# Two fp32 buffers for x and another way to place the first state, in an attention and feed-forward kernel

## The chip, the core and the metric

The kernel runs on one core of one Trainium2 chip. The metric is the device time of one execution, in microseconds. Each run has a state: it counts as slow when it is more than 1.5% above the fastest run of the same kernel, or ran at a clock lowered throughout; ratios use fast runs only. For before, whose fastest run took 218.28 us, runs up to 221.5 us still count as fast. Engines: PE multiplies matrices, PEld is its weight load, DVE the vector engine, ACT the scalar engine, POOL the general engine that also issues software DMAs, SP the engine that issues nearly all the other DMAs (its queue is shown as SPq).

## The reference, cut to what matters

```python
B, H, S, Ns, D = 8, 8, 512, 32, 64          # x: (B,H,S,D), state: (B,H,Ns,D)
scores = x @ state.T / sqrt(D);  a = softmax(scores);   xread = a @ state
scores2 = state @ x.T / sqrt(D); a2 = softmax(scores2); sread = a2 @ x
h_in = concat([xread, sread], axis=2)       # 544 rows per batch, 512 wide
g = silu(h_in @ w_in)                       # 512 -> 2048
out = g @ w_out                             # 2048 -> 512, 4352 rows
```

The kernel works batch by batch. For the 512 x rows of a batch it folds `state @ w_in` into one matrix W of the batch ("G1" multiplies by W, "G2" by w_out; `aT`, the transposed softmax weights, is the other operand of G1). `ft` counts the 16 tiles of the 2048-wide middle layer. So PE has some 23 us of dense matmuls for each batch.

## The kernel before: the parts that matter

Each batch's x travels a chain: load (DMA, fp32) into `x_f`, cast to bf16 into `x_nat`, transpose into `xT`, scores on PE. The kernel has one `x_f` buffer for all batches. Batches 0 and 1 are transposed on PE; from batch 2 on the DMA queues transpose.

```python
x_f = pers.tile([128, H, 4, D], FP32)                 # one buffer
def load_x(b, h0=0, nh=H):
    nc.gpsimd.dma_start(x_f[:, ds(h0, nh)], x[b, ...])
def transpose_x(b):
    nc.sync.dma_start_transpose(xT[b] ..., x_nat[b] ...)

# state of batch 0: one PE transpose, then four strided copies on ACT
ps0 = transpose_one_state(st0_n)
place_one_state(0, ps0, nc.scalar)
...
load_x(1, 0, 4); load_x(1, 4, 4); load_states()       # in the start
pe_transpose_a(0, 1, nc.vector, nc.scalar)            # aT copied in two halves
...
# batch 0, ft 13: cast x1 on DVE, then load x2 into the same x_f
for hg in range(2):
    cast_x(1, nc.vector, 0, 4, 4 * hg, 4)
load_x(2)
...
# batch 0, last quarter, ft 11
for c in range(4):
    cast_x(2, nc.gpsimd, c, 1)                        # POOL
transpose_x(2)                                        # SP queue
...
# batch 1, ft 12: scores of batch 2 on PE, then
if b == 1:
    load_x(3)                                         # POOL, once the casts of x2 freed x_f
```

Although `load_x(3)` is written in batch 1, POOL has nothing between it and the four casts of x2, so POOL issues it directly behind them (the trace below shows it there), long before PE comes to that point.

The softmax here doesn't subtract the row's maximum and nothing guards it: scores larger than these inputs give would overflow.

Of the kernel before, what the change touches and what calls it, by code (L numbers as in the profile page):

```python
# [8 lines left out]
FP32 = mybir.dt.float32  # L9
# [10 lines left out]
H = 8  # L20
S = 512
NS = 32
D = 64
# [18 lines left out]
def kernel(  # L42
# [8 lines left out]
    nc = tc.nc  # L51
    ds = bass.ds
# [3 lines left out]
    pers = ctx.enter_context(tc.tile_pool(name="pers", bufs=1))  # L56
# [15 lines left out]
    def bank(shape, dtype, name):  # L72
        tag = banks[turn[0] % len(banks)]
        turn[0] += 1
        return psA.tile(shape, dtype, tag=tag, name=name)

    ident = pers.tile([128, 128], BF16)
# [3 lines left out]
    st0_n = pers.tile([128, 2, D], BF16)  # L81
# [18 lines left out]
    xT = {}  # L100


    x_f = pers.tile([128, H, 4, D], FP32)

    def load_x(b, h0=0, nh=H):
        nc.gpsimd.dma_start(  # L106
            x_f[:, ds(h0, nh)], x[b, ds(h0, nh)].rearrange("h (p c) d -> p h c d", p=128, c=4)
        )

    def ones_beside_x(i, eng):  # L110
        eng.memset(
            x_rows[i][:, 0 : 16 * XW].rearrange("p (i w) -> p i w", w=XW)[:, :, 0:PAD], 1.0
        )
        eng.memset(x_rows[i][:, ds(16 * XW, PAD)], 1.0)

    def padded(b):
        return x_rows[b % NX][:, ds(PAD, 16 * XW)].rearrange(
            "p (c k w) -> p c k w", c=4, k=4
        )[:, :, :, 0:128]

    def cast_x(b, eng, c0=0, nc_=4, h0=0, nh=H):
        if b < 2:
            x_nat[b] = padded(b)
        elif b not in x_nat:
            x_nat[b] = xpool.tile([128, 4, 4, 128], BF16, tag="x_nat", name=f"x_nat{b}")
        copy(
            eng,
            x_nat[b][:, ds(c0, nc_), ds(h0 // 2, nh // 2), :].rearrange(
                "p c k (u d) -> p c k u d", u=2
            ),  # L130
            x_f[:, ds(h0, nh), ds(c0, nc_), :].rearrange("p (k u) c d -> p c k u d", u=2),
        )

    def transpose_x(b):
# [13 lines left out]
    def copy(eng, dst, src):  # L148
        if eng is nc.scalar:
            nc.scalar.activation(dst, src, func=COPY, bias=0.0)  # L150
        else:
            eng.tensor_copy(dst, src)  # L152


    def keep_busy(n, pool, tag):
        ps = pool.tile([128, 512], FP32, tag=tag, name="ps_busy")
        for _ in range(n):
            nc.tensor.matmul(  # L158
                ps[:], busy[:, 0:128], busy[:], start=True, stop=True, skip_group_check=True
            )  # L160
# [9 lines left out]
    nc.scalar.activation(warm[:], warm[:], func=EXP, bias=0.0)  # L170
    for hg in range(2):
        nc.sync.dma_start(
            x_f[:, ds(4 * hg, 4), :, :],
            x[0, ds(4 * hg, 4)].rearrange("h (p c) d -> p h c d", p=128, c=4),
        )
    nc.vector.memset(stT[:, 0], 0.0)
# [14 lines left out]
    def load_states():  # L191
        nc.gpsimd.dma_start(
            st_b[:], state.rearrange("b h (n2 m v) d -> (b h n2) m (v d)", n2=2, m=8)
        )

    def transpose_one_state(st):
        ps = bank([128, 2, 2, 2, 16], BF16, "ps_st1")
        nc.tensor.transpose(
            ps.rearrange("p g k u m -> p (g k u m)"), st.rearrange("p v d -> p (v d)"), ident[:]
        )  # L200
        return ps

    def place_one_state(b, ps, eng):
        flat = stT.rearrange("p b k s n -> p (b k s n)")
        to = (
            flat[0:64, ds(256 * b, 320)].rearrange("p (g w) -> p g w", g=2)[:, :, 0:128],
            flat[64:128, ds(256 * b + 32, 192)].rearrange("p (g w) -> p g w", g=2),
        )
        for u in range(2):
            by_n = to[u].rearrange("p g (k m v) -> p g k m v", m=16, v=2)  # L210
            for v in range(2):
                copy(eng, by_n[:, :, 0:3:2, :, v], ps[ds(64 * v, 64), :, :, u, :])

    keep_busy(7, psH, "h1")
    copy(nc.vector, st0_n[:], st0_f[:])
    ps0 = transpose_one_state(st0_n)
    keep_busy(2, psH, "h1")


# [14 lines left out]
                    )  # L234
            copy(engs[u], xT[b][:, ds(m * u, m), ds(2 * hg, 2), :], ps[:])

    place_one_state(0, ps0, nc.scalar)
    cast_x(0, nc.vector, 0, 2, 0, 4)
    cast_x(0, nc.scalar, 2, 2, 0, 4)
    new_o = lambda sh, dt, nm: psO.tile(sh, dt, tag="o", name=nm)  # L240
# [80 lines left out]
    def pe_transpose_a(b, hg, eng, other=None):  # L321
        ps = bank([128, 4, 128], BF16, "ps_at")
        for c in range(4):
            nc.tensor.transpose(ps[:, c, :], an[b, hg][:, c, :, :], ident[:])
        if other is None:
            copy(eng, aT[b][:, hg, :, :], ps[:])
        else:
            copy(eng, aT[b][:, hg, 0:2, :], ps[:, 0:2])
            copy(other, aT[b][:, hg, 2:4, :], ps[:, 2:4])
# [194 lines left out]
    for hg in range(2):  # L524
        load_x(1, 4 * hg, 4)
    load_states()
    for i in (1, 2):
        ones_beside_x(i, nc.gpsimd)
    keep_busy(4, psO, "o")
    pe_transpose_a(0, 0, nc.vector)  # L530
    keep_busy(1, psO, "o")
    pe_transpose_a(0, 1, nc.vector, nc.scalar)
    g1_half(0, 0)
    g1_half(1, 0)

# [7 lines left out]
    for ft in range(NFT):  # L543
        upto(min(ft + LEAD0[ft], ready))
        if ft in W0:
            w1_cols(0, [W0[ft]], both)
            ready = sum(W0[ft]) // 128
        if ft == 4:
            place_one_state(1, transpose_one_state(st1_n), nc.vector)
        if ft == 13:  # L550
            for hg in range(2):
                cast_x(1, nc.vector, 0, 4, 4 * hg, 4)
            load_x(2)
        if ft in (5, 9, 11):
            w1_chunks(1, ({5: 0, 9: 1, 11: 2}[ft],), both)
        if ft == 14:
            nc.scalar.activation(warm[:], warm[:], func=EXP, bias=0.0)
            pe_transpose_x(1, 0, 1, engs=(nc.vector,))
            pe_transpose_x(1, 1, 1, engs=(nc.vector,))
        if ft < 14:  # L560
            for tt in range(3):
                G2(0, tt, ft)
# [32 lines left out]
    for b in range(1, B):  # L595
        n = b + 1
        lead = 4 if b == 1 else 6
        for tt in range(4):
            for ft in range(NFT):
                at = (tt, ft)  # L600
                if tt == 0:
                    upto(NFT * b + min(lead + ft, NFT))
                if b == 1 and at == (0, 1):
                    transpose_state()
                    for u in range(2):
                        evict_state(u, nc.vector)
                if b == B - 1 and at in ((0, 4), (0, 8)):
                    place_xm(at[1] // 8, nc.vector)
                if n < B:
                    if at == (0, NFT - lead):  # L610
                        scores(n, 0)
                        scores(n, 1)
                        exps(n, 0)
                        exps(n, 1)
                        nc.scalar.activation(warm[:], warm[:], func=SILU, bias=0.0)  # L615
                        if b == 1:
                            load_x(3)
                    if at == (1, 0):
                        for hg in range(2):
                            norm(n, hg, (((nc.gpsimd, nc.vector)[hg], 0, 4),))  # L620
                            transpose_a(n, hg)
                        if n + 1 < B:
                            for c in range(4):
                                cast_x(n + 1, nc.gpsimd, c, 1)
                        if n + 2 < B:
                            load_x(n + 2)
                    if at == (3, 8):
                        if n + 1 < B:
                            transpose_x(n + 1)
                    if at == (0, 4):  # L630
                        copy(nc.vector, padded(n), x_nat[n][:])
                    if at == (2, 4):
                        if b == 1:
                            sread((0, 1))
                        sread((n,))
                        pss = w1_mms(n, [(0, 512), (512, 512)])
                        w1_out(n, [(0, 512)], both, pss)
                        for m in (0, 1, 2) if b == 1 else (n,):
                            sread_out(m)
                        w1_out(n, [(512, 512)], both, pss)  # L640
                    if at == (3, 4):
                        w1_chunks(n, (2, 3), both)
                    if tt == 3 and ft % 2 == 1 and ft // 2 < 6:
                        upto(NFT * n + ft // 2 + 1)
                elif tt > 0 and (ft % 3 == 2 or ft == NFT - 1):
                    upto(min(done[0] + 1, NFT * (B + 1)))
                G2(b, tt, ft)
            store(b, tt, nc.scalar if tt in (1, 2) else nc.vector)
        for ft in range(NFT):
            gt.pop(NFT * b + ft)  # L650
# [34 lines left out]
```

## Time and profile before

| | before |
|---|---|
| timed, median of the first 3 runs | 218.43 us (218.41 to 218.93) |
| the profiled run | 225.7 us, span 223.9 us, marked slow |
| PE busy in that run | 211.0 us, 94% |
| period of a later batch on PE | 22.91 us |

The page of before. The digits are tenths of busy time, or of the full TensorE clock, in 40 equal slices of the span:

```profile
span 223.9 us, 3944 instructions
...
PE   7799999983999999999999999999999999999993
...
PEclk9999999997699999999999999999999999999999
...
```

PE is full except at both ends and in slices 9 and 10; its clock is down in slices 10 and 11 (7 and 6 tenths). The waits view of PE (what waited, for what: us in total, times, longest) has one long wait:

```profile
...
PE ps_sc L279 <- DMA xT<-x_nat: 4.1, 1, 4.1
PE ps_busy L158 <- DVE warm L165: 1.2, 1, 1.2
...
```

The timeline around it (start us, length us, engine, line; in brackets the idle time before it and what ended it):

```profile
...
32.56 0.89 POOL L106 DMA_DIRECT2D x_f<-in_x_dram  x1 [16.29 <-DVE x_rows L152]
...
41.85 2.28 POOL L152 CAST x_nat<-x_f 128x512 bf16<-128x512 f32 x4 [3.79 <-DMA x_f<-in_x_dram]
...
44.16 1.79 SPq L137 DMA_TRANSPOSE xT<-x_nat  x1
...
44.43 0.93 POOL L106 DMA_DIRECT2D x_f<-in_x_dram  x1 [0.30 <-POOL x_nat L152]
...
53.91 1.04 PE L279 MATMUL ps_sc<-stT,xT 128*128 128x64 bf16 x16 [4.07 <-DMA xT<-x_nat]
...
```

This is the chain of x2: load issued at 32.56, after POOL had waited for the cast of x1; landed just before 41.85; four casts; transpose issued at 44.16; load of x3 issued 0.27 us later; scores of batch 2 at 53.91, after PE stood 4.07 us. The view of stretches (stretch and its length, busy us and count of PE, PEld, DVE, ACT, POOL, then granted clock, DMA share, GB/s) shows what followed:

```profile
...
45.00:50.00 5.00, 4.79 (x22) 1.99 (x21) 1.45 (x4) 4.60 (x9) 0.36 (x1) 1.00 1.22 154
50.00:55.00 5.00, 1.09 (x17) 0.99 (x18) 0.00 (x0) 2.21 (x3) 0.00 (x0) 0.80 0.64 215
55.00:60.00 5.00, 5.00 (x13) 1.77 (x12) 3.21 (x6) 2.12 (x4) 1.59 (x2) 0.52 0.15 56
...
```

The clock is 0.52 from 55 to 60 us. The Trainium skill, "TensorE: Matmul & The Clock Gate", Part 1, names a cause for a fall of this kind: PE's clock is halved after an idle window of about 3.4 us. Here PE stood 4.07 us.

The start, up to the first exp of batch 0:

```profile
...
4.50 0.99 ACT L150 ACTIVATE stT<-ps_st 64x64 bf16<-64x64 bf16 x4 [1.80 <-PE ps_st L198]
...
5.05 0.43 DVE L152 CAST x_rows<-x_f 128x512 bf16<-128x512 f32 x1 [1.04 <-DMA x_f<-in_x_dram]
...
5.51 0.63 ACT L150 ACTIVATE x_rows<-x_f 128x512 bf16<-128x512 f32 x1
...
7.44 0.60 ACT L293 ACTIVATE exp_nat<-ps_sc 128x512 bf16<-128x512 f32 x1 [0.34 <-PE ps_sc L279]
...
```

And the aT copy in front of the first G1 that waits for it:

```profile
...
10.88 0.84 DVE L152 COPY aT<-ps_at 128x512 bf16<-128x512 bf16 x2
...
11.75 0.38 ACT L150 ACTIVATE aT<-ps_at 128x256 bf16<-128x256 bf16 x1 [0.22 <-DVE aT L152]
...
12.19 0.59 PE L425 MATMUL h<-aT,W 128*128 128x512 bf16 x2 [0.24 <-ACT aT L150]
...
```

### The profile page before, as it was taken

The page shows a single profiled execution, that of the slowest core. Times are in us where ns is not written, and L with a number is a line of the kernel's source. Part 1 is how long each engine was busy: PE and PEld are TensorE (multiplying, and loading weights), DVE is VectorE, ACT ScalarE, POOL GpSimd, SP SyncE. Part 2 cuts the span into 40 slices and gives each one's busy share as a digit, 9 for nine tenths or more (in the row PEclk, how much of TensorE's full clock was granted, in tenths as well). Part 3 has the DMA queues.
Part 4 walks back from the last instruction along what each step waited for, and adds up shares of the span by engine and source line. Part 5 has one row for each costly group of instructions (what it writes and reads, how often), then busy time and mean ns, then how long its engine had stood idle before and what let it go on. Part 6 is the DMA issues. An engine that isn't in the chain of part 4 may idle for free.

```text
span 223.9 us, 3944 instructions
## 1 busy us (share of the span) xinstructions
PE 211.0 (94%) x1576; PEld 99.0 (44%) x1602; DVE 78.1 (35%) x174; ACT 143.9 (64%) x248; POOL 42.2 (19%) x65
## 2 busy tenths in 40 slices
PE   7799999983999999999999999999999999999993
PEld 2433354432344444445444443444444444466652
DVE  3724257420553236222722173206420643310011
ACT  4866678794238794879577956696669666824410
POOL 8580013410520007000800070006000100000000
PEclk9999999997699999999999999999999999999999
DMA  6999958295266313940389057703530240011112
GB/s 201 182 205 207 253 149 253 75 139 193 70 206 169 91 42 103 260 119 10 104 250 165 0 95 239 192 3 87 162 88 0 70 126 27 21 47 50 47 47 94
DMA packets 33522, 27.09 MB, mean 121 GB/s; under 512 B 21344, under 2 KB 27360, under 8 KB 33504
## 3 DMA queue, kind: packets, MB, share of 16 engines
q1 hardware_dynamic: 26384, 14.95, 24.7%
q0 software_dynamic: 6976, 11.83, 24.2%
q8 instruction: 12, 0.20, 0.4%
q10 hardware_dynamic: 144, 0.07, 0.1%
q14 instruction: 6, 0.05, 0.1%
HBM read 17.43 MB, written 8.91 MB: 118 GB/s over the span
## 4 chain that ended last, share of the span: by engine, by line
PE 74%; issue 11%; DMA 6%; POOL 3%; DVE 3%; ACT 1%; SPq 1%; POOLq 0%; ACTq 0%
PE o L465 41%; PE h L425 18%; DMA xT<-x_nat 4%; PE ps_w L392 4%; PE h L444 3%; DMA aT<-an 2%; POOL an L307 2%; PE ps_busy L158 2%; PE o_half L487 2%; PE ps_sc L279 2%; PE o_a L465 1%; PE ps_sr L344 1%; POOL x_nat L152 1%; DVE W L152 1%; PE ps_xt L230 1%
## 5 line engine op out<-in xcount | busy, mean ns | idle before, releaser
L465 PE MATMUL o<-w_out_sb,g 128*128 128x512 bf16 x494 | 135.2, 385 | 1.9 <-issue 1.1
L457 ACT ACTIVATE g<-h 128x512 bf16<-128x512 f32 (+1 forms) x145 | 82.2, 571 | 35.0 <-PE h L425 20.8
L465 PEld LDWEIGHTS <-g 128*128 128x128 bf16 x528 | 50.5, 99 | 61.6 <-issue 9.8
L425 PE MATMUL h<-aT,W 128*128 128x512 bf16 x250 | 74.5, 379 | 0.7 <-ACT aT L150 0.2
L152 DVE COPY o_sb<-o 128x512 f32<-128x512 f32 x17 | 11.7, 691 | 88.1 <-PE o L465 88.1
L425 PEld LDWEIGHTS <-W 128*128 128x128 bf16 x256 | 24.8, 98 | 31.5 <-issue 2.0
L152 DVE CAST W<-ps_w 128x512 bf16<-128x512 f32 (+1 forms) x31 | 20.5, 679 | 36.7 <-PE ps_w L392 36.7
L307 POOL TENSOR_TENSOR an<-exp_nat,rc 128x512 bf16<-128x512 bf16 (+1 forms) x9 | 9.1, 1015 | 112.2 <-ACT exp_nat L293 73.3
L150 ACT ACTIVATE o_sb<-o 128x512 f32<-128x512 f32 x15 | 8.9, 596 | 23.0 <-PE o L465 10.5
L150 ACT ACTIVATE W<-ps_w 128x512 bf16<-128x512 f32 (+1 forms) x35 | 18.7, 577 | 7.5 <-PE ps_w L392 7.4
L152 POOL CAST x_nat<-x_f 128x512 bf16<-128x512 f32 x24 | 16.0, 702 | 3.8 <-DMA x_f<-in_x_dram 3.8
L293 ACT ACTIVATE exp_nat<-ps_sc 128x512 bf16<-128x512 f32 (+1 forms) x17 | 9.0, 570 | 4.1 <-PE ps_sc L279 4.1
L392 PE MATMUL ps_w<-w_in_sb,stT 64*32 64x512 bf16 (+1 forms) x264 | 11.5, 376 | 0.0
L304 DVE TENSOR_REDUCE rs<-exp_nat 128x16 f32<-128x512 bf16 (+1 forms) x17 | 10.7, 630 | 0.9
L106 POOL DMA_DIRECT2D x_f<-in_x_dram x8 | 7.1, 894 | 17.8 <-DVE x_rows L152 16.3
L279 PE MATMUL ps_sc<-stT,xT 128*128 128x64 bf16 x128 | 6.0, 199 | 4.7 <-DMA xT<-x_nat 4.1
L444 PE MATMUL h<-xmT,w_in_sb 128*128 128x256 bf16 x64 | 9.6, 273 | 0.1
L279 PEld LDWEIGHTS <-xT 128*128 128x128 bf16 x128 | 5.2, 102 | 7.1 <-DMA xT<-x_nat 4.6
L444 PEld LDWEIGHTS <-w_in_sb 128*128 128x128 bf16 x64 | 6.3, 98 | 3.9
L293 ACT ACT_TABLE_LOAD x6 | 7.7, 1283 | 0.1
L615 ACT ACT_TABLE_LOAD x6 | 7.7, 1283 | 0.1
L158 PE MATMUL ps_busy<-busy 128*128 128x512 bf16 x15 | 6.1, 530 | 1.3 <-DVE warm L165 1.2
(57 smaller groups left out, 92.0 us busy)
## 6 DMA issues: line engine op xcount, KB each, us to landing
out_dram<-o_sb SPq DMA_DIRECT2D x33, 256.0 KB, 2.5
x_f<-in_x_dram POOLq DMA_DIRECT2D x6, 1024.0 KB, 8.0
w_in_sb<-in_moe_w_in_dram POOLq DMA_DIRECT2D x3, 512.0 KB, 10.6
w_out_sb<-in_moe_w_out_dram POOLq DMA_DIRECT2D x3, 512.0 KB, 12.4
x_f<-in_x_dram SPq DMA_DIRECT2D x2, 512.0 KB, 4.7
x_f<-in_x_dram POOLq DMA_DIRECT2D x2, 512.0 KB, 17.1
w_in_sb<-in_moe_w_in_dram POOLq DMA_DIRECT2D x2, 256.0 KB, 7.0
w_out_sb<-in_moe_w_out_dram POOLq DMA_DIRECT2D x2, 256.0 KB, 7.5
```

Source lines behind the costliest of these rows:

```text
L150: nc.scalar.activation(dst, src, func=COPY, bias=0.0)
L152: eng.tensor_copy(dst, src)
L158: nc.tensor.matmul(ps[:], busy[:, 0:128], busy[:], start=True, stop=True, skip_group_check=True)
L279: nc.tensor.matmul(sc_ps[hg][-1][:, c % m, ds(2 * j, 2), :], xT[b][:, c, 2 * hg + j, :], stT[:, b, 2 * hg + j, :, :], start=True, stop=Tru ...
L293: nc.scalar.activation(e[:, ds(n * i, n)], ps[:], func=EXP, bias=0.0, scale=SCALE)
L304: nc.vector.tensor_reduce(rs[:, ds(c, nr)], e[:, ds(c, nr)], axis=AX, op=ADD)
L307: eng.tensor_tensor(a[:, ds(c, n)], e[:, ds(c, n)], rc[:, ds(c, n)].to_broadcast([128, n, 4, NS]), op=MULT,)
L392: nc.tensor.matmul(pss[f, hg][ds(32 * s, 32), 0:n], stT[ds(r, 64), b, h // 2, s % 2, :], w_in_sb[ds(r, 64), h // 2, ds(f, n)], start=True, ...
L425: nc.tensor.matmul(h_ps[k][:], W1[b][:, hg, ds(128 * ft, 128)], aT[b][:, hg, :, :], start=(hg == 0), stop=(hg == 1), skip_group_check=True,)
L444: nc.tensor.matmul(ps[:, 0:256], w_in_sb[:, kt, ds(128 * ft, 128)], xmT[:, :, kt].rearrange("p t n b -> p t (n b)"), start=(kt == 0), stop ...
L457: nc.scalar.activation(g[:, ds(i, m)], ps[:, ds(i, m)], func=SILU, bias=0.0)
L465: nc.tensor.matmul(outs[tt][:], gt[b * NFT + ft][:, ds(128 * tt, 128)], w_out_sb[:, ft, :], start=(ft == 0), stop=(ft == NFT - 1), skip_gr ...
```

## The change

The intent: with two buffers, the load of x2 can stand in the queue right behind the loads of the states, and need not wait until x1 has been cast; the state of batch 0 needs two copies instead of four and leaves ACT free for its cast of x. A third part, not named in the intent, leaves the second aT copy of batch 0 to DVE alone.

```diff
-    x_f = pers.tile([128, H, 4, D], FP32)
+    x_f = [pers.tile([128, H, 4, D], FP32, name=f"x_f{i}") for i in range(2)]
...  (x_f becomes x_f[b % 2] in load and cast)
-    ps0 = transpose_one_state(st0_n)
+    ps0 = bank([128, 4, 16, 2], FP32, "ps_st0")
+    by_head = ident.rearrange("p (k u m) -> p k u m", u=2, m=16)
+    for v in range(2):
+        for u in range(2):
+            nc.tensor.matmul(ps0[ds(64 * u, 64), :, :, v], st0_n[:, v, :],
+                by_head[:, :, u, :], start=True, stop=True,
+                tile_position=(0, 64 * u), skip_group_check=True)
...
-    place_one_state(0, ps0, nc.scalar)
+    for u in range(2):
+        copy(nc.vector, slots_of(0)[u] ..., ps0[ds(64 * u, 64)] ...)
...
     load_states()
+    load_x(2)
...
-    pe_transpose_a(0, 1, nc.vector, nc.scalar)
+    pe_transpose_a(0, 1, nc.vector)
...
                 cast_x(1, nc.vector, 0, 4, 4 * hg, 4)
-            load_x(2)
+            load_x(3)
...
-                        if b == 1:
-                            load_x(3)
```

The load of x3 moves too, from behind the casts of x2 to before them.

More of the change, by code (lines that the diff above doesn't have):

```diff
@@ L100 @@
     xT = {}
-    x_f = pers.tile([128, H, 4, D], FP32)
+    x_f = [pers.tile([128, H, 4, D], FP32, name=f"x_f{i}") for i in range(2)]
     def load_x(b, h0=0, nh=H):
         nc.gpsimd.dma_start(
-            x_f[:, ds(h0, nh)], x[b, ds(h0, nh)].rearrange("h (p c) d -> p h c d", p=128, c=4)
+            x_f[b % 2][:, ds(h0, nh)],
+            x[b, ds(h0, nh)].rearrange("h (p c) d -> p h c d", p=128, c=4)
         )
@@ L130, in cast_x @@
             ),
-            x_f[:, ds(h0, nh), ds(c0, nc_), :].rearrange("p (k u) c d -> p c k u d", u=2),
+            x_f[b % 2][:, ds(h0, nh), ds(c0, nc_), :].rearrange("p (k u) c d -> p c k u d", u=2),
         )
@@ L172 @@
         nc.sync.dma_start(
-            x_f[:, ds(4 * hg, 4), :, :],
+            x_f[0][:, ds(4 * hg, 4), :, :],
             x[0, ds(4 * hg, 4)].rearrange("h (p c) d -> p h c d", p=128, c=4),
@@ L201, in transpose_one_state, with slots_of @@
         return ps
-    def place_one_state(b, ps, eng):
+    def slots_of(b):
         flat = stT.rearrange("p b k s n -> p (b k s n)")
-        to = (
+        return (
             flat[0:64, ds(256 * b, 320)].rearrange("p (g w) -> p g w", g=2)[:, :, 0:128],
@@ L208, in place_one_state @@
         )
+    def place_one_state(b, ps, eng):
         for u in range(2):
-            by_n = to[u].rearrange("p g (k m v) -> p g k m v", m=16, v=2)
+            by_n = slots_of(b)[u].rearrange("p g (k m v) -> p g k m v", m=16, v=2)
             for v in range(2):
@@ L215 @@
     copy(nc.vector, st0_n[:], st0_f[:])
-    ps0 = transpose_one_state(st0_n)
+    ps0 = bank([128, 4, 16, 2], FP32, "ps_st0")
+    by_head = ident.rearrange("p (k u m) -> p k u m", u=2, m=16)
+    for v in range(2):
+        for u in range(2):
+            nc.tensor.matmul(
+                ps0[ds(64 * u, 64), :, :, v],
+                st0_n[:, v, :],
+                by_head[:, :, u, :],
+                start=True,
+                stop=True,
+                tile_position=(0, 64 * u),
+                skip_group_check=True,
+            )
     keep_busy(2, psH, "h1")
@@ L235, in pe_transpose_x @@
             copy(engs[u], xT[b][:, ds(m * u, m), ds(2 * hg, 2), :], ps[:])
-    place_one_state(0, ps0, nc.scalar)
+    for u in range(2):
+        copy(
+            nc.vector,
+            slots_of(0)[u].rearrange("p g (k n) -> p g k n", n=NS)[:, :, 0:3:2, :],
+            ps0[ds(64 * u, 64)].rearrange("p (g k) m v -> p g k (m v)", g=2),
+        )
     cast_x(0, nc.vector, 0, 2, 0, 4)
```

## The prediction

> **What bounds the kernel.** TensorE. The page gives PE 211.0 of 223.9 us (94%), and the chain of waits gives PE 74%. From batch 2 on, the chain repeats a PE-only period: scores of successive batches start at 79.99 and 102.90 us, and at 149.02 and 171.93 us, 22.91 us apart. Nothing in the change touches those periods.
>
> **The wait that the change aims at.** In the profiled run the scores of batch 2 start at 53.91 us, after PE stood 4.07 us for the DMA transpose of x (the waits view of PE; it is PE's only long one). Chain: cast of x1 ends 32.26, load of x2 issued by POOL 32.56 (POOL had stood 16.3 us for that cast), POOL casts x2 from 41.85 (after 3.79 us for the load) to 44.14, transpose lands 53.86. After the idle time the granted clock is 0.52 in 55–60 us (stretches view). The Trainium skill, "TensorE: Matmul & The Clock Gate", Part 1, says that an idle window of about 3.4 us halves the clock; the trace agrees. The step from these scores to the next ones takes 26.08 us instead of 22.91; some 0.6 us of that is the 64 extra state-read matmuls, so the low clock cost about 2.5 us.
>
> **But the timed runs are not this run.** The profiled run took 225.7 us and is marked slow; timed ones take 218.43. The gap, 7.3 us, is about the wait plus the clock loss (4.07 + 2.5 = 6.6). So I think the timed runs already have next to no wait there (0 to 0.7 us), and most of what the profile promises is not in the metric.
>
> **What the change does.**
> 1. The load of x2 follows the states, at about 15.6 us on POOL, into its own buffer. I expect landing at 36 to 38 us behind x1 (31.5) and the states (32.6) instead of 41.8. POOL then casts right after its normalisation (38.06), to about 40.4; the transpose starts some 3.7 us earlier, with most of the load of x3 out of its way, and lands at about 44 to 48, before PE needs it (49.8). Profile: 4.1 us of wait and 2.5 us of low clock go. Timed: 0 to 0.7 us.
> 2. Batch 0's state: four ACT copies (4.50–5.49, 0.24 us each) become two DVE copies (estimate 0.25 us each), and one transpose becomes four small matmuls (estimate +0.2 us). ACT's cast of x starts when its load lands (5.05, not 5.51), DVE's about 0.1 us later. The second transposed x was copied at 6.63; I expect 0.13 us earlier.
> 3. The aT copy on DVE alone (0.42 us) replaces DVE 0.29, a handover and ACT 0.38 in series: 0.27 us less before the first G1 (12.19).
> Steps 2 and 3 give 0.4 us at 12 us, but the start is fed by DMA: PE already waits 0.44 us for w_in at 20.99, and DVE waits 0.32 and 0.68 us for x1 at 30.2 and 31.6. I expect half or more to be given back there.
>
> **Prediction.** Timed: 217.7 us, range 215.9 to 218.6. Profiled run: span about 217, one undisturbed clock. Chances: faster by over 2% 0.06, within 2% 0.91, slower by over 2% 0.03.
>
> **What would show it.** Right: no PE wait for xT at the scores of batch 2, clock 1.0 throughout, first G1 at about 11.8, scores of batch 1 earlier by under 0.3 us, later periods still 22.9 us.
>
> **What would make it wrong.** If timed runs do wait up to 3 us (too short for the clock to fall), the gain is up to 3.5 us. If the x2 load in the start slows x1 or the weights, the start lengthens. If the transpose still collides with loads and stores, the wait stays.

## The result, and the profile after

| | before | after |
|---|---|---|
| timed, 4 runs each, median | 218.68 us (218.41 to 219.09) | 218.70 us (218.40 to 218.89) |
| ratio of fast runs | | 0.9998 (0.9975 to 1.0021) |
| the profiled run | 225.7 us, slow | 218.89 us, fast |

A ratio is the mean time of one kernel's fast runs over that of the other's in the same rounds, so it is not quite the ratio of the medians.

The page of after:

```profile
span 217.0 us, 3946 instructions
...
PE   7799999999999999999999989999999999999993
...
PEclk9999999999999999999999999999999999999999
...
```

The waits view of PE, after:

```profile
...
PE ps_busy L159 <- DVE warm L166: 1.2, 1, 1.2
...
PE h L445 <- DMA aT<-an: 0.4, 1, 0.4
...
```

The chain of x2, after (two pieces of the timeline; the first line is now the load of x3):

```profile
...
32.05 0.88 POOL L106 DMA_DIRECT2D x_f<-in_x_dram  x1 [12.50 <-DVE x_rows L153]
...
37.78 2.28 POOL L153 CAST x_nat<-x_f 128x512 bf16<-128x512 f32 x4
...
40.08 1.70 SPq L138 DMA_TRANSPOSE xT<-x_nat  x1
...
```

```profile
...
49.44 0.63 PE L299 MATMUL ps_sc<-stT,xT 128*128 128x64 bf16 x16
...
```

The wait for xT is gone and the clock stays up. The scores of batch 2 start at 49.44 us and wait for nothing. The load of x2 itself was issued at 17.99 us on POOL and landed 17.1 us later, at 35.1.

The start, after:

```profile
...
4.75 0.59 DVE L153 CAST stT<-ps_st 64x128 bf16<-64x128 f32 x2 [0.74 <-PE ps_st L223]
5.17 0.63 ACT L151 ACTIVATE x_rows<-x_f 128x512 bf16<-128x512 f32 x1 [2.48 <-DMA x_f<-in_x_dram]
...
5.37 0.43 DVE L153 CAST x_rows<-x_f 128x512 bf16<-128x512 f32 x1
...
7.43 0.60 ACT L313 ACTIVATE exp_nat<-ps_sc 128x512 bf16<-128x512 f32 x1 [0.24 <-PE ps_sc L299]
...
```

```profile
...
10.88 0.97 DVE L153 COPY aT<-ps_at 128x512 bf16<-128x512 bf16 x2
...
11.35 1.14 PE L445 MATMUL h<-aT,W 128*128 128x512 bf16 x4
...
```

The profile looks as the change intended, and its span is 6.9 us shorter than that of before. The timed runs are the same. Two questions follow: what do the fast runs of before look like, and where did the small gains in the start go?

### The profile page after: what moved, and what is told of

Same layout as the page of the kernel before. It is cut to its first block, busy times and chain, and to the rows that moved or that the text cites. A ratio compares the mean times of both kernels' runs of the same rounds, so it can differ in the third digit from the quotient of the medians.

```text
span 217.0 us, 3946 instructions
## 1 busy us (share of the span) xinstructions
PE 208.1 (96%) x1579; PEld 98.0 (45%) x1605; DVE 78.5 (36%) x176; ACT 142.5 (66%) x243; POOL 42.0 (19%) x65
## 4 chain that ended last, share of the span: by engine, by line
PE 82%; issue 10%; DVE 2%; DMA 2%; POOL 2%; SPq 1%; POOLq 0%
PE o L485 43%; PE h L445 23%; PE ps_w L412 4%; PE h L464 3%; DMA aT<-an 2%; PE ps_busy L159 2%; PE o_half L507 2%; PE ps_sc L299 2%; PE o_a L485 1%; PE ps_sr L364 1%; POOL an L327 1%; DVE W L153 1%; PE ps_xt L245 1%; PE ps_at L344 1%; SPq L337 1%
## 5 line engine op out<-in xcount | busy, mean ns | idle before, releaser
L485 PE MATMUL o<-w_out_sb,g 128*128 128x512 bf16 x494 | 132.8, 380 | 1.9 <-issue 1.1
L485 PEld LDWEIGHTS <-g 128*128 128x128 bf16 x528 | 49.8, 98 | 60.1 <-issue 7.0
L327 DVE TENSOR_TENSOR an<-exp_nat,rc 128x512 bf16<-128x512 bf16 (+1 forms) x8 | 6.7, 831 | 0.3
```

The costliest lines, as they stand in the source:

```text
L327: eng.tensor_tensor(a[:, ds(c, n)], e[:, ds(c, n)], rc[:, ds(c, n)].to_broadcast([128, n, 4, NS]), op=MULT,)
L485: nc.tensor.matmul(outs[tt][:], gt[b * NFT + ft][:, ds(128 * tt, 128)], w_out_sb[:, ft, :], start=(ft == 0), stop=(ft == NFT - 1), skip_gr ...
```

## The experiments

All outputs are right. Each experiment's rounds also ran the kernel before, so before was timed 50 times in all, counting e1.

### e1: before again

No edit.

> The kernel before, unchanged, to get a second profile of it. Theory A (the timed runs of before have no wait for the transposed x of batch 2; the 4.07 us wait and the low clock belong to slow executions only): a fast profile of about 217.1 us shows PE waiting under 0.5 us for xT at the scores of batch 2, clock 1.0, ratio 1.000. Rival B (fast runs wait too, up to 3 us, just without the clock loss, and the change gives its gain back elsewhere): a fast profile shows a wait of 1 to 3 us there. If the profile is slow again it shows the 4 us wait, and only tells that the wait comes often.

Measured: 6 runs of 218.56 to 223.29 us, ratio of fast runs 1.0008 (0.9943 to 1.0074). This time the profile fell on a fast run (218.56 us), of 216.8 us span:

```profile
...
38.48 2.28 POOL L152 CAST x_nat<-x_f 128x512 bf16<-128x512 f32 x4 [0.44 <-DMA x_f<-in_x_dram]
...
40.79 1.79 SPq L137 DMA_TRANSPOSE xT<-x_nat  x1
...
41.06 0.93 POOL L106 DMA_DIRECT2D x_f<-in_x_dram  x1 [0.30 <-POOL x_nat L152]
...
49.85 0.52 PEld L279 LDWEIGHTS <-xT 128*128 128x128 bf16 x16 [0.52 <-DMA xT<-x_nat]
...
```

The idle time on the last line is that of the weight load, PEld; the waits view has no PE wait for xT at all. How long the transpose took from issue to landing is on the line of DMA issues:

```profile
...
xT<-x_nat SPq DMA_TRANSPOSE x1, 9.0
```

So this fast run of before has next to no wait, and it has nothing to spare either: the transpose, issued at 40.79, lands 9.0 us later, at 49.8, just when PE comes for it. It costs a little even so: from the scores of batch 1 to those of batch 2 this trace takes 15.80 us (34.06 to 49.86), and the traces of after, e2 and e10, where the transpose lands early, take 15.60. What differs in the slow profile is the load of x2: 9.2 us from issue to landing there, 6.5 us here. In the slow profile of e3 it took 8.8 us. Theory A holds for this run. But before is not one time: 2 of these 6 runs, and 10 of all 50 runs of before, were over 220 us. Mean clock: the five of the ten that count as slow (223.25 to 226.14 us) have 0.983 to 0.990, the other five (220.43 to 221.44 us, still counted as fast) 0.997 to 1.0. That fits a short wait in the latter and a longer wait with the low clock in the former, but none of these ten was traced; the slow profiles of before and e3 are the evidence for it.

### e2: only the two buffers and the earlier loads

The `x_f` hunks and the moved loads of the diff, nothing else.

> Only the two x buffers and the earlier loads. Theory A: same time as before, ratio 0.998 to 1.002, because nothing waited; the transpose of x2 lands near 46 us instead of after 49. Rival B: faster by 1 to 3 us (0.986 to 0.995). Either way no run in the slow state with a wait at the scores of batch 2.

Measured: 218.43 to 218.93 us in 6 runs, ratio of fast runs 0.996 (0.9915 to 1.0005). The line of the transpose:

```profile
...
xT<-x_nat SPq DMA_TRANSPOSE x1, 3.7
```

It is issued at 40.32 and lands at 44.0, and the scores follow without a wait:

```profile
...
49.68 0.63 PE L279 MATMUL ps_sc<-stT,xT 128*128 128x64 bf16 x16
...
```

Against the fast run of before the transpose starts only 0.5 us earlier; it takes 3.7 us instead of 9.0. I had expected a landing near 46. The ratio cannot tell A from B, since the fast runs of before beside it include two over 221 us. But the lowest runs are level (218.43 here, 218.59 in before), which is what A says, and the spread is far smaller than that of before.

### e3: only the state of batch 0

The `ps0` and copy hunks of the diff.

> Only the state of batch 0 by four matmuls and two vector copies. Theory: no gain, ratio 0.999 to 1.001, because the vector engine takes the two copies (0.59 us) in front of its own cast of x and both engines meet again at the second xT copy; exp of batch 0 starts at 7.4 us as before. Rival (what I predicted): 0.13 us earlier at the exp.

Measured: 218.43 to 222.95 us, 3 of 6 runs over 220 us, ratio of fast runs 1.001 (0.9945 to 1.0076). The exp of batch 0 starts at 7.44 us, as in before (7.44). The theory holds: ACT's cast of x starts at 5.14 instead of 5.51, but DVE has the two state copies (0.59 us) in front of its own cast, which starts at 5.38 instead of 5.05. Both xT copies run on DVE, and its next cast of x starts at 6.97 in both kernels. One trace could not show 0.13 us by the exp alone: it starts at 7.28 in e10 and at 7.58 in e14, which have this part of before unchanged.

This profile fell on a slow run, with a PE wait for xT of only 2.54 us. The stretches from 52 us (columns as above):

```profile
...
52.00:54.00 2.00, 1.63 (x20) 0.93 (x21) 0.00 (x0) 1.16 (x3) 0.00 (x0) 0.84 0.10 30
54.00:56.00 2.00, 2.00 (x6) 0.76 (x5) 1.69 (x4) 1.41 (x2) 0.00 (x0) 0.50 0.07 28
56.00:58.00 2.00, 2.00 (x9) 0.80 (x8) 1.53 (x3) 0.00 (x0) 1.99 (x2) 0.80 0.28 103
...
```

The clock fell here too, after a wait well under the 3.4 us that the Trainium skill names, in the same place. The step to the next scores took 24.73 us instead of 23.13 in e1, so it cost 1.6 us.

### e4: only the aT copy

> Only the aT copy of batch 0 on the vector engine alone. Theory: first gated G1 0.25 to 0.3 us earlier, and kept, because the loads follow PE rather than lead it: scores of batch 1 0.2 us earlier, ratio 0.999 (0.2 us of 218.4). Rival (predicted): half or more given back at the weight loads, under 0.1 us left.

Measured: 218.12 to 219.39 us in 6 runs, ratio of fast runs 0.9964 (0.9917 to 1.001). The scores of batch 1 start at 33.78 us, against 34.06 in e1, and those of batch 2 at 49.50 against 49.86: the gain of 0.28 us at batch 1 is kept through the loads. But later, between the scores of batches 5 and 6 in this trace, a period takes 23.18 us instead of 22.91. In before it takes 23.20, in after 23.48, in e13 (after again) 23.37; in after the waits view names the wait, 0.4 us for the transpose of aT, and the timeline has it at 129.1 us (in e13, 0.29 us at the same place is put down to a copy on ACT). In e1 and e2 it takes 22.92 and 22.91. That loss comes and goes between runs whichever parts of the change are in, and it is as large as the gain. I did not find its cause.

### e5, e6, e7: the chain of x2 made longer

```diff
-            for c in range(4):
-                cast_x(2, nc.gpsimd, c, 1)
+            for _ in range(2):            # e6: range(3)
+                for c in range(4):
+                    cast_x(2, nc.gpsimd, c, 1)
             transpose_x(2)
```

e5 and e6 do this to before, e7 (twice) to after.

> Before, with the four POOL casts of x2 done twice, which starts the transpose of x2 some 2.3 us later. The result stays right. Theory (in fast runs of before the transposed x2 lands just as PE asks for it, with under 0.5 us to spare): the fast time rises by about 2 us, to 220.5 to 221.5 us, and the profile shows a PE wait for xT of 2 to 3 us at the scores of batch 2. Rival (fast runs have several us to spare and the slow ones are another disturbance): no rise.

Measured: 220.12 to 220.87 us in 4 runs, ratio of fast runs 1.0087 (1.0061 to 1.0113). PE waits 1.56 us for xT at the scores of batch 2, the clock stays at 1.0, and the other periods are unchanged. The casts took 4.51 us instead of 2.28; of the 2.2 us more, about 0.7 were covered because the load had landed a little earlier (the casts began at 38.11, not 38.48) and the transpose took 8.7 us instead of 9.0. The waits view:

```profile
...
PE ps_sc L279 <- DMA xT<-x_nat: 1.6, 1, 1.6
...
```

The wait is shorter than the 2 to 3 us that I expected, but the kernel pays for it: that shows, on fast runs, that before has nothing to spare there.

> Before, casts of x2 done three times, some 4.6 us later. Theory (wait plus the clock that falls after a long idle time): every run near 225 to 226 us, as the slow profile of before: wait of about 4.5 us and some us at clock 0.5, in all 6.5 to 7.5 us more than 218.6. If the low clock has another cause: only 4.5 us more, about 223 us.

Measured: 222.30, 226.19, 226.68 and 227.67 us. The profile is of the 227.67 us run: a wait of 6.22 us, more than I expected, since the load of x2 was late as well (the casts began at 40.00) and the transpose took 10.0 us, and a step to the next scores of 25.28 us, so 2.2 us lost to the clock. The mean clock is 0.983, 0.991, 0.992 and 0.985 in the four runs, so it fell in all of them, also in the run of 222.30 us; why that one lost so little is not known, since only the first was traced.

> After, with the same doubled casts. Theory (the change gives the transpose about 3 us to spare at this place, which no fast run needs): time unchanged, 218.2 to 219 us, no PE wait for xT over 0.3 us. If the two buffers gave no room: 2 us more.

Measured: 218.12 to 218.89 us, ratio of fast runs 0.9991 (0.996 to 1.0022), no PE wait for xT. The same 2.2 us cost after nothing: its transpose was issued at 42.25 and landed 3.8 us later, over 3 us early.

### e8, e9: the load of x3 put back beside the transpose

After, with only `load_x(3)` moved back to where before has it; x2 stays early.

```diff
-            load_x(3)                      # batch 0, ft 13
...
+                        if b == 1:         # batch 1, behind the casts of x2
+                            load_x(3)
```

> After, but the load of x3 put back to where before has it, on POOL behind the casts of x2, so that it runs with the transpose of x2 again. Theory (the room comes from the early load of x2): the transpose starts at 40 us, takes 8 to 9.5 us instead of 7.3 or less, lands by 49.6, time unchanged within 0.3 us, but with less to spare. Rival (the collision of the transpose with the load of x3 makes the slow runs): runs of 220 us and more come back, and the profile shows a wait for xT.

Measured: 226.49 to 228.13 us in 4 runs, all of them, ratio 1.0382 (1.034 to 1.0424). I had not expected it: the rival was right, and more than right. The chain of x2, the time of the transpose and PE's wait for it:

```profile
...
38.02 2.28 POOL L153 CAST x_nat<-x_f 128x512 bf16<-128x512 f32 x4
...
40.25 0.93 POOL L106 DMA_DIRECT2D x_f<-in_x_dram  x1
40.33 2.12 SPq L138 DMA_TRANSPOSE xT<-x_nat  x1
...
```

```profile
...
xT<-x_nat SPq DMA_TRANSPOSE x1, 16.2
```

```profile
...
PE ps_sc L299 <- DMA xT<-x_nat: 6.7, 1, 6.7
...
```

x2 is as early as in after, the transpose starts as early as in after, and it takes 16.2 us instead of 3.8. PE waits 6.67 us and the clock falls. Here the load finds its buffer free, and is issued 0.08 us before the transpose; in before it has to wait for the last cast's signal, and comes 0.27 us behind it. e9 tests this by one 0.33 us memset on POOL in front of the load:

```diff
                         if b == 1:
+                            nc.gpsimd.memset(idle_t[:, 0:256], 0.0)
                             load_x(3)
```

> As e8 (x2 early, load of x3 behind the casts of x2), with one POOL memset of 0.33 us in front of that load, so that the transpose is issued first, as in before (there by 0.27 us). Theory (what matters is which of the two enters the DMA queues first): the transpose lands in about 9 us, near 49.3, as in before, and the fast time is 218.2 to 219 us, against 226.6 in e8. Rival (any overlap of these two in this place costs 16 us): about 226 us again.

Measured: 219.66, 220.16 and 220.26 us. The profiled run took 274.23 us because the granted clock was 0.756 over the whole span, so its times on PE say nothing here; its transpose took 10.3 us, with the load issued 0.17 us behind it. So a quarter of a microsecond of delay for the load goes with about 6 us less for the transpose and 6.5 us less for the kernel. That fits the theory that it matters who is first, though the time stayed over the 218.2 to 219 us that I had written. That 10.3 us is too long by about 1 us would account for it, but no undisturbed trace shows it.

The Trainium skill, "DMA: Bandwidth & Descriptors", section "Queues, rings and completion order", says that each DMA engine goes round between the queues that it has work for, one packet at a time. That the two slow each other fits it. It gives no figure for a load against a transpose, and doesn't say that the order of two issues 0.1 to 0.3 us apart is worth 6 us. Sharing alone does not account for e8 either: one after the other, in e10 below, the transpose took 3.8 us and the load of x3 6.2 us, 10.0 us together, and e8 took 16.2. What the rest is stays open.

### e10: one buffer, but the load of x3 kept away from the transpose

Before, with four POOL memsets of about 1 us in front of the load of x3.

```diff
                         if b == 1:
+                            for _ in range(4):
+                                nc.gpsimd.memset(idle_t[:, 0:1024], 0.0)
                             load_x(3)
```

> Before, with one x buffer, and four POOL memsets of about 1 us in front of the load of x3, so that the transpose of x2 runs alone. Theory (the collision with the load of x3 is what uses up the slack, not the late load of x2): the transpose lands in about 3.8 us, at 44 to 47 us, every run is fast (218.3 to 219.0 us), none over 220, as with the two buffers. Rival (the late load of x2 is the cause): slow runs of 220 us and more stay as frequent as in before, about one in four.

Measured: 218.38 to 219.88 us in 6 runs, none over 220 (but one, 219.88, above the 219.0 that I expected), ratio of fast runs 0.9981 (0.9941 to 1.0021); of the 11 runs of before beside it, two were over 220 (221.35 and 224.10).

```profile
...
39.11 2.28 POOL L152 CAST x_nat<-x_f 128x512 bf16<-128x512 f32 x4 [0.78 <-DMA x_f<-in_x_dram]
...
41.34 3.97 POOL L619 MEMSET idle_t<- 128x1024 bf16 x4
41.42 1.69 SPq L137 DMA_TRANSPOSE xT<-x_nat  x1
...
45.26 0.93 POOL L106 DMA_DIRECT2D x_f<-in_x_dram  x1
...
```

```profile
...
xT<-x_nat SPq DMA_TRANSPOSE x1, 3.8
```

With one buffer, and x2 loaded as late as in before, the transpose takes 3.8 us, as in after. So what uses up the slack of before is the overlap with the load of x3.

### e11, e12: can the start be made to gain?

e11 is after with one state copy on DVE and one on ACT; e12 also drops the two filler matmuls (meant to keep PE's clock up) that lie in the start's chain of waits.

```diff
     for u in range(2):
         copy(
-            nc.vector,
+            (nc.vector, nc.scalar)[u],
...  (e12 only)
-    keep_busy(1, psH, "h1")
     pe_transpose_x(0, 1, 2, new_h, (nc.vector, nc.scalar))
...
-    keep_busy(1, psO, "o")
     pe_transpose_a(0, 1, nc.vector)
```

> After, with the two state copies on two engines (vector and scalar). Theory (the two copies in front of the vector engine's cast took the gain): cast of x on both engines from about 5.1 to 5.2 us, exp of batch 0 0.1 to 0.25 us earlier than in after, time 0.998 to 0.9995 of before. Rival (the arrival of the second half of x, about 6.5 us, sets the exp): exp at 7.4 us as in all kernels.

Measured: 217.97 to 218.69 us, ratio of fast runs 0.9953 (0.9911 to 0.9994). The exp of batch 0 starts at 7.51 us; the split did not bring it forward in this trace, against the theory. ACT's copy started only at 5.07, and its wait is put down to DVE's copy into the same tile (4.76 plus 0.28), so the two still ran one after the other.

> As e11, and without the two filler matmuls that the chain of waits of after shows in the start (0.22 us each, at 7.4 and 10.8 us). If the clock stays up: first G1 0.4 us earlier than in e11, time 0.996 to 0.999 of before. If the fillers are needed: a stretch at clock 0.5 in the first 20 us and a time up to 2 us longer.

Measured: 218.19 to 218.49 us, ratio of fast runs 0.9956 (0.9919 to 0.9993). The clock stayed up, but the first G1 starts at 11.28 us, against 11.43 in e11 and 11.35 in after, and PE then waits 0.21 us for w_in at 21.0 us: the scores of batch 1 start at 34.05, later than in after (33.84). These two ratios are the only ones of the fast versions whose interval leaves out 1, but the fast runs of before beside them include one of 221.35 us, and after did not run in those rounds. A gain over after is not shown for either.

### e13, e14, e15: more runs

e13 is after unchanged, e14 is after without the state part, e15 is e10 with the aT copy on DVE.

> After, unchanged. Theory (the change removes the slow runs and about 0.2 us): no run over 220 us, mean about 218.6, while the runs of before beside it have one in five over 220 us and a mean near 219.7. Rival (the slow runs of before are the chip's and not the kernel's): as many runs over 220 us as before.

Measured: 218.28 to 218.67 us in 6 runs, ratio of fast runs 0.9975 (0.9945 to 1.0004). The 11 runs of before beside it had two over 220 us (220.43 and 223.25).

> After without the state part. Theory (the state part gives nothing): same as e13 within 0.15 us in the mean, exp of batch 0 at 7.4 us, first G1 0.25 us earlier than in before.

Measured: 218.11 to 218.83 us, ratio of fast runs 0.9972 (0.9942 to 1.0002), so the state part gives nothing that these runs can show (after in e13: 0.9975).

> Before with one x buffer, the load of x3 behind four POOL memsets, and the aT copy on the vector engine alone. Theory (keeping the load of x3 off the transpose is enough): no run over 220 us, mean 218.5 to 218.9. Rival (the second buffer is needed): runs over 220 us.

Measured: 218.13 to 219.06 us, ratio of fast runs 0.9979 (0.9945 to 1.0012), none over 220. These runs do not need the second buffer.

Taken together:

| where the load of x3 goes | kernels | runs | over 220 us | highest |
|---|---|---|---|---|
| 0.27 us behind the start of the transpose | before (with e1), e3, e4 | 62 | 13 | 226.14 us |
| before the casts of x2 | after (with e13), e2, e7, e11, e12, e14 | 38 | 0 | 218.93 us |
| 4 us behind it, one buffer | e10, e15 | 12 | 0 | 219.88 us |

If runs over 220 us came at the first row's rate, 13 in 62, whatever the kernel, 38 runs would have none with a chance of about 1 in 8000, and 12 runs with one of about 1 in 17 (my estimate from these counts). So for e10 and e15 the short transpose in e10's trace says more than the count.

After alone, in 10 runs, has a mean of 218.56 us (218.28 to 218.89). Before, in 50 runs, has 10 over 220 us; the other 40 have a mean of 218.86. No version was clearly faster than after: e14, with a little less code, is as fast.

## Why the prediction was wrong

The prediction gave 217.7 us, 215.9 to 218.6; measured were 218.70 us, no change.

- **What bounds the kernel: right.** The later periods stay at 22.91 us in every trace but that of e9, which ran at a low clock; the exception is the step from batch 5 to batch 6, told below.
- **Point 1, the profile is a slow run and the fast ones hardly wait: right.** e1 shows no PE wait for xT in a fast run of before. The term of 0 to 0.7 us that I still counted for it is about 0.2 us in that trace (15.80 us from the scores of batch 1 to those of batch 2, against 15.60 in after) and 0.1 in e4's (15.72).
- **Point 1, why the transpose would land earlier: right in direction, wrong in weight.** I put the gain on the start, 3.7 us earlier. Against a fast run of before the start is 0.7 us earlier (40.08 against 40.79), and the duration does the rest: 3.8 us instead of 9.0. I had named the load of x3 only in half a sentence ("with most of the load of x3 out of its way"). e8 and e10 show that this is the cause: x2 early and x3 beside the transpose is 8 us slower than before; x2 late and x3 away from it has a transpose of 3.8 us and no run over 220 us either.
- **Point 2, 0.13 us from the state: not seen.** e3 has the exp at 7.44, as before. I followed ACT's cast and forgot that DVE, which now has the copies, also has a cast to do and both xT copies behind it. The copies themselves cost what I estimated (0.59 us for two, against 0.5).
- **Point 3, 0.27 us from the aT copy: right.** The first SiLU after it starts at 12.31 us in after and at 12.60 in before, and in e4 the scores of batch 1 come 0.28 us earlier.
- **The step that failed** is the sum at its end: what is kept of the gain, and where the rest is lost. I wrote 0.4 us at 12 us, half or more of it given back to the loads of the start, plus 0 to 0.7 us for the wait. (With half given back and the middle of the wait that is 0.55 us, so 217.9; 217.7, which is 0.73 us below 218.43, is reached only with nothing given back.) The loads took nothing: the scores of batch 5 still come 0.38 us earlier in after (118.43) and 0.52 us earlier in e13 (118.29) than in e1 (118.81). What I did not have is the step from these to the scores of batch 6. It takes 23.48 us in after and 23.37 in e13, and 22.92 in e1, and so takes back all or nearly all: batch 6 starts at 141.91, 141.66 and 141.73. e7, which has every part of the change, takes 22.92 us there, and its span is 216.3 us against 216.8 in e1. That the timed runs lose the gain in the same place is not shown, since they have no traces.
- **The size is small against the scatter.** After's own 10 runs lie between 218.28 and 218.89 us, and e13 alone has a median of 218.50. The 218.43 us from which I subtracted was the median of three runs; the 40 runs of before that are not over 220 us have a mean of 218.86. Against that, after's mean is 0.30 us lower; the ratio of e13, 0.9975, has an interval that still holds 1.
- **What I did not see** is that before is not one time. "Most of what the profile promises is not in the metric" is true of a median of fast runs. One run of before in five, 10 of 50, is over 220 us; the first comparison drew none. The traces of before and e3 put this down to the wait of the profile. There the change does what its profile shows: 10 runs, none over 218.89.

Three things stay open: why the load of x2 takes 6.5 us in some executions of before and 8.8 to 9.2 in others, what sets the later wait, and why a load just in front of the transpose costs more than the two take apart.

## What to carry to other kernels

When a profile shows a wait that the timed runs don't have, look for a chain that lands with nothing to spare: here it hardly moved the median, but made a share of slow runs, and doubling one link of the chain (e5, e7) measures the slack in timed runs. When a transfer on the critical chain is slow, look first at what shares the DMA queues with it in those microseconds: moving the other transfer was worth 5 us of duration here, while starting earlier was worth 0.7. When copies go from one engine to another, add up the whole queue of the engine that gets them.

## What the Trainium skill lacked or had wrong

- "DMA: Bandwidth & Descriptors" has no figure for a DMA transpose that shares the queues with a load. Here the same transpose of 512 KB took 3.7 to 3.9 us with no load of x issued beside it, 8.7 to 10.3 us with a 1 MB software load issued 0.17 to 0.27 us behind it (10.3 in e9's run at a low clock), and 16.2 us with the load issued 0.08 us in front of it.
- The same page, "Latency and other measured facts", gives 261 GB/s for a DMA transpose with a non-contiguous middle dimension. From issue to landing, with no load of x in flight, 512 KB in 3.8 us is 138 GB/s here (524,288 bytes over 3.8 us); this time holds the latency too, so it does not show the page to be wrong.
- "TensorE: Matmul & The Clock Gate", Part 1, has an idle window of about 3.4 us before the clock is halved, and says that the window runs freely. Here a wait of 2.54 us was enough once (e3: clock 0.50 from 54 to 56 us), and one of 1.56 us was not (e5). PE had work again from 52.37 us in e3, and the clock was still 1.00 from 52 to 53 us, so the window of 3.4 us before the fall was not an idle one throughout. A wait of 2.5 us is not safe.
- No page that I read says when POOL, with DMA loads queued, holds back the next one. In after, POOL issued the load of x2 at 17.99 us, after 1.94 us of waiting for an earlier w_out load to land, though the buffer was free; it cost nothing here. Whether the chip or the compiled program asks for that wait is not shown.
